# Attention and mixture of experts: whole-token scratch with one gather a tile, and single indirect transfers in the attention

## The chip, the cores and the metric

The kernel runs on one core of a Trainium2 chip. The metric is device time in microseconds (us): the median of several executions. The kernel before takes 1117.5 us (median of 3, 1113.73 to 1119.49).

The core's engines are TensorE (PE, with its weight loads as PEld), VectorE (DVE), ScalarE (ACT), GpSimd (POOL) and SyncE (SP), which issues most of the DMAs. Each engine takes its instructions in the order of the program; between engines they wait for one another by semaphores.

## The reference

```python
# q, k, v: 8 batches x 8 heads x 576 x 64
mask_plain = (rel >= 0) & (rel < 32)                      # heads 0..3
mask_dil = (rel >= 0) & (rel < 128) & (rel % 4 == 0)      # heads 4..7
attn = softmax(where(mask, q @ k.T / 8, -1e9))
x = (attn @ v).transpose(0, 2, 1, 3).reshape(4608, 512)   # one row a token

logits = x @ w_gate                                       # 8 experts
noisy = logits + log1p(exp(x @ w_noise)) * noise
top2 = argpartition(-noisy, 2, axis=1)[:, :2]
w = softmax(noisy[top2])
out = 0
for e in range(8):
    for k in range(2):
        m = top2[:, k] == e
        out[m] += w[m, k] * (relu(x[m] @ w1[e]) @ w2[e])  # 512 -> 1024 -> 512
```

## The kernel before, in words

**Attention.** The 8 batches make four units of two, and each unit has a dilated group (heads 4 to 7) and a plain one (heads 0 to 3). Each group is worked in three steps, 24 in all. A loop of 26 rounds, each with two half steps, works several steps at once in a pipeline. For a step, `qk` (L345) computes the scores on PE (L362); VectorE takes the maximum (L367) and subtracts it (L368) into a tile `a`, of which there is one; `expo` is ScalarE's exponential (L373); `ptr` transposes on PE (L387) and copies on ScalarE (L388); `pv` multiplies by v on PE (L405) and divides on VectorE (L412 to L417) into a tile `x`; `store_x` sends `x` from SP to a scratch in device memory, `xs` (L430, L432). `x_transpose` (L440) and `gate_mm` (L462) give the gate's logits, which ScalarE copies to their tokens' columns (L467 for plain heads, L488 for dilated ones).

The scratch of before has 9216 rows of 256 numbers: half a token each (the plain half or the dilated one), in the order in which the steps make them. `setup_b` (L220 to L252) computes on VectorE, from a token's number, the rows of its two halves, and `tokc` holds both.

**The table.** Generators run beside the attention, some instructions at a time. They pick each token's two experts, count their places, and write an entry (the two rows, the weight, the token) into a table `tab` in device memory, sorted by expert. `fill_slots` (L619) does that on GpSimd, with one indirect DMA of 128 rows for each of 36 token tiles and each of the two choices: 72 scatters. Those of the second choice go through a list, `backlog`, and are popped from it when there is room.

**The pace of the indirect transfers.** `new_slot` gives a number of turns at every half step: 4, 0, 4, 0 and so on. Each scatter of the table and each tile's gather in the attention takes one turn, in `pool_turn`. Ahead of the transfer, `pace` puts a tiny instruction on GpSimd: for the first turn of a slot a copy of one element of the latest `x` into `spacer` (L297), so that GpSimd waits there until that `x` exists, and for the other turns a memset (L299), which waits for nothing of PE or VectorE.

**Experts.** For each of the 8 experts, up to 1216 token rows are worked in three blocks of 3, 4 and 2 or 3 tiles of 128. `up` (L802) multiplies by w1 on PE (L814), with the relu on ScalarE (L818) into `hh` and the rest of a split into two parts on VectorE (L820); `down` (L841) multiplies by w2 (L856, and L850 and L852 for a last short tile), scales on VectorE (L865), and GpSimd adds the rows to the output with an indirect DMA (L833). Weights are loaded by SP into staging tiles `ws`, two of each kind (L686 for w1, L700 for w2), then split by ScalarE and VectorE.

Rows for expert 0 are gathered in the attention's last part, two indirect DMAs a tile (L758, one for each half token), and transposed on PE. Those of a later expert are gathered with four indirect DMAs a tile (L766), each of 32 tokens by four quarters of 128 numbers, so that the tile lies ready for VectorE's transposes in squares of 32 (L783), ScalarE's copy (L785) and VectorE's subtraction (L786). Their indices are loaded by SP (L735, L738, L740) and worked out on GpSimd (`idx_copy`, L742).

**A planner** sets the order in the experts: `plan` (L884) puts a function at a time in us of PE work, and `tick` (L892) advances that clock after each group of matmuls and emits what is due. `plan_x` (L794) plans, for a block's tile, its gather at a time t and its split at t + `LAG` (15). During expert 0 a function `some` gives one turn in each of the first 36 us to the rest of the table's scatters, and the backlog follows behind.

Of the kernel before, what the change touches and what calls it, by code (L numbers as in the profile page):

```python
# [41 lines left out]
LAG = 15  # L42
US_X = (17, 52)
# [3 lines left out]
def attention_moe_kernel(ctx, tc, qt, kp, kd, vpl, vdl, w_gate, w_noise, noise, w1, w2, out, CAPS=(1216, 1216, 1216, 1184, 1184, 1152, 1152, 1152), SPLITS=(0, 384, 896)):  # L47
# [49 lines left out]
    VD = dp.tile([128, 2, 9, 4, 2, 65], F32, name="vd")  # L97
# [15 lines left out]
    def v_loads(g):  # L113
        u, ty = g // 2, 1 - g % 2
        if ty:
            d = VD.rearrange("p w j h y c -> p w (j h y c)")
# [61 lines left out]
    for ty in range(2):  # L178
        eng = vector if ty == 1 else gpsimd
        m = acon.tile([128, 18, 64], BF, name=f"mask{ty}")  # L180
        eng.tensor_copy(m, m0[:, 0:1].to_broadcast([128, 18, 64]))
        if ty == 1:
            for blk, kd_ in {0: 1, 9: 1, 4: 2, 13: 2, 5: 3, 14: 3}.items():
                eng.tensor_copy(m[:, blk], m0[:, kd_])
        else:
            for x in range(2):
                for h in range(2):
                    p0 = 64 * x + 32 * h
                    eng.tensor_copy(m[p0:p0 + 32, 6 * h], m0[p0:p0 + 32, 1])
        masks.append(m)  # L190
# [29 lines left out]
    def setup_b():  # L220
# [3 lines left out]
        gpsimd.iota(tokc[:, :, 3:4], pattern=[[128, NT], [0, 1]], base=0, channel_multiplier=1)  # L224
        t = tokc[:, :, 3]
        v, s, i0, z, a = (acon.tile([128, 2, NT], I32, name=f"tc{i}") for i in range(5))
        gpsimd.iota(v[:, 0].rearrange("p (s j) -> p s j", j=3), pattern=[[0, 12], [128, 3]], base=0, channel_multiplier=1)
        vector.tensor_scalar(a[:, 0], t, 2, None, op0=OP.bitwise_and)
        vector.tensor_scalar(v[:, 1], t, 2, None, op0=OP.logical_shift_right)
        vector.scalar_tensor_tensor(v[:, 1], a[:, 0], 72.0, v[:, 1], op0=OP.mult, op1=OP.add)  # L230
        for u in range(U):
            c = slice(NG * u, NG * u + NG)
            gpsimd.iota(s[:, 0, c].rearrange("p (s j) -> p s j", j=3), pattern=[[384, 3], [0, 3]],
                        base=384 * (6 * u + 3), channel_multiplier=0)
            vector.tensor_scalar(a[:, 0, c], t[:, c], float(TU * u + S), 144.0, op0=OP.is_ge, op1=OP.mult)
            vector.scalar_tensor_tensor(v[:, 1, c], v[:, 1, c], -288.0 * u, a[:, 0, c], op0=OP.add, op1=OP.add)
            vector.memset(s[:, 1, c], 2304 * u)
        for lim in (192.0, 384.0):
            vector.tensor_scalar(z[:, int(lim) // 384], v[:, 1], lim, None, op0=OP.is_ge)
        vector.tensor_tensor(z[:, 0], z[:, 0], z[:, 1], op=OP.add)  # L240
        vector.scalar_tensor_tensor(s[:, 1], z[:, 0], 384.0, s[:, 1], op0=OP.mult, op1=OP.add)
        vector.tensor_scalar(a[:, 0], t, 1, None, op0=OP.bitwise_and)
        vector.tensor_tensor(z[:, 0], a[:, 0], z[:, 0], op=OP.subtract)
        vector.scalar_tensor_tensor(v[:, 1], z[:, 0], 192.0, v[:, 1], op0=OP.mult, op1=OP.add)

        vector.tensor_tensor(i0, v, s, op=OP.add)
        vector.tensor_scalar(a, v, 31, None, op0=OP.bitwise_and)
        vector.tensor_tensor(i0, i0, a, op=OP.add)
        vector.tensor_scalar(a, v, 32, None, op0=OP.bitwise_and)
        vector.scalar_tensor_tensor(i0, a, -31.0 / 32, i0, op0=OP.mult, op1=OP.add)  # L250
        for c in range(2):
            vector.tensor_copy(tokc[:, :, c], i0[:, c])  # L252
# [26 lines left out]

    gens, early = [], [True]  # L280
    room, held, rate = [0], set(), [1]
# [12 lines left out]
    def pace(yes=True):  # L294

        if yes and late["x"] is not None:
            gpsimd.tensor_copy(spacer, late["x"])  # L297
# [3 lines left out]
    def pool_turn():  # L301


        pace(fresh[0] and not experts[0])
# [31 lines left out]
    def blocks(st, ty):  # L336

        for r in range(6):
            a, jp = divmod(r, 3)
            b, ub = divmod(12 * st + 2 * r, 18) if ty == 0 else divmod(6 * st + 2 * jp, 9)  # L340
            yield r, a, jp, b, ub

    SB, PE_, PT, XG, XT, GS = {}, {}, {}, {}, {}, {}

    def qk(k):  # L345
# [8 lines left out]
        for e in range(6):  # L354
            for qd in range(4):
                if ty == 0:
                    x = qd // 2
                    b, ub = divmod(12 * st + 6 * (qd % 2) + e, 18)
# [10 lines left out]
        SB[k] = a  # L369

    def expo(k):
        p = sm.tile([128, 6, 64, 2], F32, name="pe")
        scalar.activation(p.rearrange("p j c w -> p j w c"), SB.pop(k).rearrange("p y (j w) c -> p (y j) w c", w=2),  # L373
                          AF.Exp, scale=0.125)
# [16 lines left out]
    def pv(k):  # L391
        g, st = divmod(k, 3)
        ty = 1 - g % 2
        pt = PT.pop(k)
        o = aps.tile([128, 2, 512], F32, name="o", tag="o")
        for hh in range(4):
            for r, a, jp, b, ub in blocks(st, ty):
                qd, c0 = (r, hh) if r < 4 else (2 * (r - 4) + hh // 2, 4 + hh % 2)
                if ty == 0:
                    y, src = hh // 2, 2 * (hh % 2) + a  # L400
                    rhs = VP[b][:, :, ub // 2, hh]
                else:
                    y, src = a, hh
                    rhs = VD[:, :, 3 * st + jp, hh, y]
                tensor.matmul(o[32 * qd:32 * qd + 32, c0 // 3, 130 * (c0 % 3):130 * (c0 % 3) + 130],  # L405
                              lhsT=pt[:, y, 128 * jp + 32 * src:128 * jp + 32 * src + 32],
# [14 lines left out]
        late["x"] = x[0:1, 0, 0, 0:1]  # L421
# [4 lines left out]

# [795 lines left out]
```

## Time and profile before

| | |
|---|---|
| device time, median of 3 (range) | 1117.5 us (1113.73 to 1119.49) |
| span of the profiled execution | 1109.4 us |
| PE busy | 1015.0 us, 91% |
| POOL busy | 527.7 us, 48% |
| DVE busy | 463.9 us, 42% |
| ACT busy | 319.8 us, 29% |
| moved by DMA | 132.91 MB, mean 120 GB/s |

The span reaches from the first instruction to the last in one profiled execution, and it is the time that the views divide. A row of the table of stretches gives, for a window of the span, each engine's busy time with its count of instructions in brackets, then the clock that the throttle granted to PE (1.00 is full speed), the mean busy share of the 16 DMA engines, and GB/s. A row of the timeline gives the start, the duration, the engine, the line, the operation, the tiles and their shapes, and in square brackets how long the engine was idle ahead of it and what released it. A row of the groups by line gives the count, then busy time and mean duration in ns, then the idle time ahead of the group's instructions and its main releaser.

### The profile page before, as it was taken

What the parts mean: (1) busy time and instruction counts of PE and PEld (TensorE: products, weight loads), DVE (VectorE), ACT (ScalarE), POOL (GpSimd) and SP (SyncE); (2) the same over time, 40 slices, a digit from 0 to 9 for tenths busy, and PEclk for the clock granted to TensorE, in tenths of its full rate; (3) what the DMA queues carried; (4) which work ended last, traced back from release to release, by engine and by line L of the source; (5) the groups of instructions that cost most, each with busy time, mean ns of one, the idle gap of its engine ahead of it and who ended that gap; (6) DMA issues with size and microseconds to landing.
All of it is one profiled execution on the core that took longest, in us unless ns stands there. A gap on an engine that the chain in (4) does not pass through costs nothing. (4 is left out here: it accounts for less than half of the span.)

```text
span 1109.4 us, 18401 instructions
## 1 busy us (share of the span) xinstructions
PE 1015.0 (91%) x7278; PEld 853.6 (77%) x7279; DVE 463.9 (42%) x1060; ACT 319.8 (29%) x612; POOL 527.7 (48%) x723
## 2 busy tenths in 40 slices
PE   5896776686999899999999999999999999999996
PEld 3774655465779789878988898788978898888885
DVE  6773535644224444334433433434343344333221
ACT  6673433531113232222222222212231213222110
POOL 6004243356866545664635564455456455553112
PEclk9998887887999999999999999999999999999999
DMA  7798687465243432633353334333433443353123
GB/s 275 254 345 292 193 270 251 122 205 161 44 90 76 102 101 48 139 60 103 65 117 68 97 72 101 82 79 85 97 83 81 104 68 102 62 129 58 32 30 46
DMA packets 77530, 132.91 MB, mean 120 GB/s; under 512 B 29968, under 2 KB 39616, under 8 KB 76160
## 3 DMA queue, kind: packets, MB, share of 16 engines
q1 hardware_dynamic: 55088, 92.55, 26.3%
q0 software_dynamic: 22352, 39.15, 19.6%
q8 instruction: 58, 0.95, 0.4%
q14 instruction: 32, 0.26, 0.1%
HBM read 92.11 MB, written 39.54 MB: 119 GB/s over the span
## 5 line engine op out<-in xcount | busy, mean ns | idle before, releaser
L814 PE MATMUL up<-x,w1h 128*128 128x512 f32 (+4 forms) x1536 | 397.5, 345 | 8.8 <-DVE hl L820 5.8
L766 POOL DMA_INDIRECT g<-xs,ixi x258 | 264.5, 1025 | 84.5 <-issue 79.1
L814 PEld LDWEIGHTS up<-x,w1h 128*128 128x128 f32 x1536 | 272.7, 189 | 36.4 <-DVE hl L820 7.6
L814 PE MATMUL up<-x,w1l 128*128 128x384 f32 (+4 forms) x768 | 264.1, 344 | 1.8 <-DVE w1l L696 1.1
L856 PE MATMUL dn<-w2h,hh 128*128 128x512 f32 x576 | 226.7, 394 | 2.0 <-DVE y L865 1.3
L856 PE MATMUL dn<-w2h,hl 128*128 128x512 f32 x576 | 225.3, 391 | 1.1 <-issue 1.1
L856 PE MATMUL dn<-w2l,hh 128*128 128x512 f32 x576 | 225.5, 391 | 0.6 <-issue 0.6
L820 DVE SCALAR_TENSOR_TENSOR hl<-up,hh 128x384 fp32r<-128x384 f32 (+2 forms) x192 | 106.1, 556 | 228.0 <-ACT hh L818 177.1
L833 POOL DMA_INDIRECT out_rows<-y,ixs x67 | 107.8, 1609 | 189.3 <-DVE y L865 158.3
L818 ACT ACTIVATE hh<-up 128x384 fp32r<-128x384 f32 (+4 forms) x192 | 94.2, 498 | 274.7 <-PE up L814 193.9
L814 PEld LDWEIGHTS up<-x,w1l 128*128 128x128 f32 x768 | 145.7, 190 | 14.7 <-DVE w1l L696 1.8
L856 PEld LDWEIGHTS dn<-w2h,hh 128*128 128x128 f32 x576 | 109.0, 189 | 25.6 <-DVE y L865 2.4
L856 PEld LDWEIGHTS dn<-w2h,hl 128*128 128x128 f32 x576 | 108.8, 189 | 24.0 <-issue 1.1
L856 PEld LDWEIGHTS dn<-w2l,hh 128*128 128x128 f32 x576 | 109.0, 189 | 22.6 <-issue 0.8
L865 DVE TENSOR_SCALAR y<-dn,ixs 128x512 f32<-128x512 f32 x63 | 46.9, 748 | 143.4 <-PE dn L856 114.9
L785 ACT CAST x<-xr 128x512 fp32r<-128x512 f32 x67 | 40.5, 605 | 189.9 <-DVE xr L783 158.5
L619 POOL DMA_INDIRECT tab<-en,si x72 | 72.2, 1002 | 30.7 <-issue 16.4
L696 DVE TENSOR_TENSOR w1l<-ws,w1h 128x1024 fp32r<-128x1024 f32 x32 | 38.8, 1217 | 94.8 <-ACT w1h L694 61.6
L297 POOL COPY spacer<-hh 1x1 f32<-1x1 f32 x72 | 24.2, 336 | 102.0 <-ACT hh L818 101.7
L694 ACT CAST w1h<-ws 128x1024 fp32r<-128x1024 f32 x32 | 33.0, 1048 | 115.9 <-DMA ws<-in_moe_w 115.8
L786 DVE TENSOR_TENSOR x<-xr,x 128x512 fp32r<-128x512 f32 x67 | 44.7, 666 | 18.0 <-ACT x L785 15.9
L783 DVE STREAM_TRANSPOSE xr<-g 128x512 f32<-128x512 f32 x67 | 45.7, 682 | 0.0
(184 smaller groups left out, 856.0 us busy)
## 6 DMA issues: line engine op xcount, KB each, us to landing
ws<-in_moe_w SPq DMA_DIRECT2D x64, 512.0 KB
out_rows<-zero SPq DMA_DIRECT2D x38, 256.0 KB
vd<-in_vdl SPq DMA_DIRECT2D x24, 390.0 KB
vp<-in_vpl SPq DMA_DIRECT2D x16, 585.0 KB
qt<-in_qt SPq DMA_DIRECT2D x14, 576.0 KB
xs<-x SPq DMA_DIRECT2D x24, 256.0 KB
kt<-in_kd SPq DMA_DIRECT2D x16, 320.0 KB
g<-xs,ixi POOLq DMA_INDIRECT x258
```

What stands on the lines that cost most here:

```text
L619: ins = gpsimd.indirect_dma_start(out=tab, out_offset=bass.IndirectOffsetOnAxis(ap=si[:, kq, t:t + 1], axis=0), in_=en[:, kq, t], in_offse ...
L696: return lambda: vector.tensor_tensor(b, s, a.bitcast(F32), op=OP.subtract)
L766: gpsimd.indirect_dma_start(out=g[:, j], out_offset=None, in_=xq, in_offset=bass.IndirectOffsetOnAxis(ap=IX[e][1][:, r0 // 32 + j:r0 // 32 ...
L783: vector.transpose(xr[:, :, 0:rn].rearrange("p c (g t) -> p g c t", t=32), g[:, 0:n].rearrange("p g (c d) -> p g c d", d=32))
L785: scalar.copy(xh[:, :, o:o + rn], xr[:, :, 0:rn])
L786: return lambda: vector.tensor_tensor(xl[:, :, o:o + rn], xr[:, :, 0:rn], xh[:, :, o:o + rn].bitcast(F32), op=OP.subtract)
L814: tensor.matmul(p[:, 0:n], lhsT=a[:, 128 * f:128 * f + 128], rhs=b[:, kc, 0:n], start=(i == 0), stop=(i == 11))
L818: scalar.activation(hh[:, f, 0:n], p[:, 0:n], AF.Relu)
L820: vector.scalar_tensor_tensor(hl[:, f, 0:m], p[:, 0:m], 0.0, hh[:, f, 0:m].bitcast(F32), op0=OP.max, op1=OP.subtract)
L833: ins = gpsimd.indirect_dma_start(out=out, out_offset=bass.IndirectOffsetOnAxis(ap=sc[0:rn, t, 1:2], axis=0), in_=y[0:rn], in_offset=None, ...
L856: tensor.matmul(p[0:rn], lhsT=a[:, f, o:o + rn], rhs=b[:, f % 2], start=(i == 0), stop=(i == 23))
L865: vector.tensor_scalar(y[0:rn], p[0:rn], wsc, None, op0=OP.mult)
```

## The change

**Scratch.** `xs` has 4608 rows of 512 numbers: whole tokens, in their own order. An entry of the table holds the token's number, so that `setup_b` loses its chain on VectorE. The host lays out q, k and v so that a step's output falls on such rows: the plain stores stay 3 DMAs a step, and the dilated ones are 3 or 4. The copies of the gate's logits become contiguous for plain heads, and those of dilated heads go from 56 to 32.

**Gather, hop.** A tile is gathered with one indirect DMA of whole tokens into `gr` (3 buffers). For expert 0 this tile is transposed on PE as before. For the later experts, SP stores it into a piece of device memory, `hop` (3 buffers; `send`, L715), and loads it back with four DMAs as squares of 32 tokens into `g` (2 buffers; `fetch`, L724). `plan_x` plans the send 4.0 us after the gather and the fetch 7.5 us after it; the split stays at `LAG`, 15, and is 11 and 13 for expert 1's first two blocks. Each split counts its rows in `full`, and before a block's `up` the planner's clock is advanced until its rows are all split. Index loads take a whole tile `ix` of table entries, and `idx_copy` goes.

**Pace.** In the attention each half step has one turn (`new_slot(1)`), and the transfer stands behind a copy of one element of `late["e"]`: the latest of `a` (set in `qk`), `x` (in `pv`) and, in the experts, `hh` (in `up`). In the experts every third turn has that copy, and the others a memset. `some` gives a turn for each 1.4 us of the planner's clock, over 78 us. The backlog is also popped in the experts, and expert 1's index load is planned 78.2 us after expert 0's start, where it stood at 42.

**First weights.** w1 of the experts is laid out by the host in the order in which the kernel loads it, so that `stage_w1` reads contiguous blocks.

The core of the diff:

```diff
-    xs = dram.tile([6 * U * 384, 256], F32, name="xs")
-    xq = xs.rearrange("r (q d) -> (r q) d", d=128)
+    xs = dram.tile([T, DM], F32, name="xs")
+    hop = ctx.enter_context(tc.tile_pool(name="hop", bufs=3, space=DRAM))
...
-            while room[0] > 0 and backlog and not experts[0]:
+            while room[0] > 0 and backlog:
...
-        pace(fresh[0] and not experts[0])
+        pace(fresh[0] if not experts[0] else turns[0] % 3 == 0)
+        turns[0] += experts[0]
...
+        late["e"] = a[0:1, 0, 0, 0:1]
...
-        late["x"] = x[0:1, 0, 0, 0:1]
+        late["e"] = x[0:1, 0, 0, 0:1]
...
+        gpsimd.indirect_dma_start(out=g[0:rn], out_offset=None, in_=xs[0:rows],
+                                  in_offset=bass.IndirectOffsetOnAxis(ap=IX[e][0:rn, t, 0:1], axis=0))
...
+    def send(e, t):
+        m = hop.tile([128, DM], F32, name="hop")
+        sync.dma_start(m[0:rn], GT[e, t][0:rn])
+    def fetch(e, t):
+        g = gp_.tile([128, 4, 128], F32, name="g", bufs=GBUFS[1])
+        for c in range(4):
+            sync.dma_start(g[32 * c:32 * c + 32, 0:rn // 32],
+                           m[0:rn, 128 * c:128 * c + 128].rearrange("(j t) d -> t j d", t=32))
...
+            plan(t + step * i + US_HOP[0], lambda ti=ti: send(e, ti))
+            plan(t + step * i + US_HOP[1], lambda ti=ti: fetch(e, ti))
...
-        new_slot((4, 0)[kb % 2], 1 if kb < 28 else 2)
+        new_slot(1, 1 if kb < 28 else 2)
...
+    def some(us=1.0):
+        credit[0] += us / US_POOL
+        if credit[0] >= 1:
+            credit[0] -= 1
+            new_slot(1)
...
+                while full.get((e, bi), 0) < BLS[e][bi][3]:
+                    tick(240)
```

On GpSimd in the attention, the first scatters of the table stand before like this (COPY is the spacer that waits for `x`, MEMSET the spacer that waits for nothing of PE or VectorE):

```order
L297 COPY spacer<-x 1x1
L619 DMA tab<-en_1453,si_1521 37376x4
L299 MEMSET spacer 1x1
L619 DMA tab<-en_1453,si_1521 37376x4
L299 MEMSET spacer 1x1
L619 DMA tab<-en_1453,si_1521 37376x4
L299 MEMSET spacer 1x1
L619 DMA tab<-en_1453,si_1521 37376x4
L297 COPY spacer<-x 1x1
```

The same place in the changed kernel:

```order
L273 COPY spacer<-x 1x1
L592 DMA tab<-en_1407,si_1475 37376x4
L273 COPY spacer<-x 1x1
L592 DMA tab<-en_1407,si_1475 37376x4
L273 COPY spacer<-a 1x1
L592 DMA tab<-en_1407,si_1475 37376x4
L273 COPY spacer<-x 1x1
L592 DMA tab<-en_1407,si_1475 37376x4
L273 COPY spacer<-a 1x1
```

Four scatters behind one wait have become one scatter behind each wait, by turns for `x` and for `a`.

On SP, between the loads of one expert's weights and the next index load, stands before (`ws` are staging tiles of weights, `ixt` and `ixs` the pieces of the index tile):

```order
L686 ISA
L686 DMA ws<-in_moe_w 128x1x1024
L735 ISA
L735 DMA ixt<-tab 32x37x2
L738 ISA
L738 DMA ixs<-tab 128x9x2
L740 ISA
L740 DMA ixs<-tab 32x2
L700 ISA
L700 DMA ws_6223<-in_moe_w 128x2x512
```

And in the changed kernel:

```order
L659 ISA
L659 DMA ws<-in_moe_w 128x1024
L715 DMA hop<-gr 128x512
L724 DMA g<-hop 32x4x128 x4
L659 ISA
L659 DMA ws<-in_moe_w 128x1024
L659 ISA
L659 DMA ws<-in_moe_w 128x1024
L715 DMA hop<-gr 128x512
L724 DMA g<-hop 32x4x128 x4
L715 DMA hop<-gr 128x512
L724 DMA g<-hop 32x4x128 x4
```

The sends and fetches of the hop now stand between the weight loads in SP's one order.

More of the change, by code (lines that the diff above doesn't have):

```diff
@@ L186, in attention_moe_kernel @@
             for x in range(2):
[L187 to L189 removed]
+                for b in range(2):
+                    eng.tensor_copy(m[64 * x:64 * x + 32, 7 * b], m0[64 * x:64 * x + 32, 1])
         masks.append(m)
@@ L223, in setup_b @@
         gpsimd.memset(tokc, 0)
[L224 to L252, printed above, removed]
+        for c in (0, 3):
+            gpsimd.iota(tokc[:, :, c:c + 1], pattern=[[128, NT], [0, 1]], base=0, channel_multiplier=1)
     def setup_c():
@@ L278, in setup_c @@
             at(6 + 6 * i, lambda i=i: pads(NR * i // 3, NR * (i + 1) // 3))
+    late["e"] = None
     gens, early = [], [True]
-    room, held, rate = [0], set(), [1]
+    room, held, rate, turns = [0], set(), [1], [0]
     fresh, backlog = [True], []
@@ L294, in pace @@
     def pace(yes=True):
-        if yes and late["x"] is not None:
-            gpsimd.tensor_copy(spacer, late["x"])
+        if yes and late["e"] is not None:
+            gpsimd.tensor_copy(spacer, late["e"])
         else:
@@ new lines, in new_idx, with idx_dma, gather @@
+        IX[e] = ixp.tile([128, nt, TC], I32, name="ix")
+    def idx_dma(e, a, b, base=None):
+        ti, n = IX[e], b - a
+        src = tab[a:b] if e == 0 else tab[bass.ds(EID[e] * ET if base is None else base, n)]
+        t, k = a // 128, n // 128
+        if k:
+            sync.dma_start(ti[:, t:t + k], src[0:128 * k].rearrange("(g t) c -> t g c", t=128))
+        if 128 * k < n:
+            sync.dma_start(ti[0:n - 128 * k, t + k], src[128 * k:n])
+    X, GT, full = {}, {}, {}
+    def gather(e, t):
+        rn = TLS[e][t][1] if e != "o" else 128
+        g = gp_.tile([128, DM], F32, name="gr", bufs=GBUFS[0])
+        rows = T
+        if e == 0:
+            rows = TU * (next((i for i in range(U - 1) if sum(TLS[0][t]) <= SPLITS[i]), U - 1) + 1)
+        elif e != "o":
+            pace()
+        gpsimd.indirect_dma_start(out=g[0:rn], out_offset=None, in_=xs[0:rows],
+                                  in_offset=bass.IndirectOffsetOnAxis(ap=IX[e][0:rn, t, 0:1], axis=0))
+        GT[e, t] = g
@@ L806, in up @@
         xh, xl = X_
+        assert full.pop(key if type(key) is tuple else (key, 0)) == n
         m = n - stacked
@@ L940, in split_first @@
     def split_first(bi, t):
+        if (0, t) not in GT:
+            later(1, lambda: split_first(bi, t))
+            return
         xsplit(0, bi, t)()
@@ L1032, in attention_moe_kernel, with drain @@
     gens.append(gate(33, 3))
-    def some():
-        new_slot(1)
+    credit = [0.0]
+    def some(us=1.0):
[3 more added lines that the diff above has]
+            new_slot(1)
+        else:
+            held.clear()
         micro(6)
-    def drain():
-        while gens:
-            some()
+    def drain(all):
+        while gens or (all and backlog):
+            some(US_POOL)
     actx.close()
-    late["x"] = None
+    late["e"] = None
     late["wp2"] = ctx.enter_context(tc.tile_pool(name="wp2", bufs=1, reuse_waits="tile"))
@@ L1158, in attention_moe_kernel @@
                 idx_dma("o", 0, 128, r0 + s0)
-                idx_copy("o", 0, 128)
                 gather("o", 0)
+                send("o", 0)
+                fetch("o", 0)
                 new_x("o", 0)
@@ L1211 @@
     given = _layouts(inputs["q"], inputs["k"], inputs["v"])
-    given.update((name, inputs[name]) for name in _NAMES)
+    given.update((name, _first_weights(inputs[name]) if name == "moe_w1" else inputs[name]) for name in _NAMES)
     for name, a in given.items():
```

212 lines of the change are left out of this document (79 added, 133 removed).

## The prediction, before the run

> **What bounds the kernel now.** First the page's head and a table of stretches: when is TensorE (PE) full, and at what clock?
>
> ```profile
> span 1109.4 us, 18401 instructions
> ```
>
> ```profile
> core 0: us, PE busy (x) PEld busy (x) DVE busy (x) ACT busy (x) POOL busy (x), PEclk, DMA share, GB/s
> 16.00:89.00 73.00, 65.87 (x1483) 53.36 (x1482) 51.78 (x177) 45.91 (x114) 5.99 (x23) 1.00 0.89 305
> 89.00:236.00 147.00, 100.55 (x1632) 74.62 (x1624) 66.58 (x245) 62.72 (x155) 55.34 (x97) 0.83 0.67 212
> 236.00:365.00 129.00, 117.14 (x558) 99.09 (x557) 49.38 (x161) 25.25 (x47) 86.32 (x129) 0.93 0.45 117
> 461.00:570.00 109.00, 106.73 (x522) 91.64 (x521) 45.87 (x75) 27.53 (x46) 61.74 (x77) 1.00 0.41 89
> ```
>
> From 461 on PE is busy 98% of the time at clock 1.00: the later experts are PE work, and nothing but a new wait changes them. The loose time lies earlier. The attention's second part, 89 to 236, has PE busy 68% of the time, at clock 0.83. Expert 0 (236 to 365) takes 129 us where a later expert with about as many matmuls takes 109. So I look at the attention's beat: each of its 24 steps has one L367, read from VectorE's timeline.
>
> ```profile
> 59.10 0.96 DVE L367 TENSOR_REDUCE mx<-s 128x12 f32<-128x768 f32 x1 [1.03 <-PE s L362]
> 65.11 0.96 DVE L367 TENSOR_REDUCE mx<-s 128x12 f32<-128x768 f32 x1 [1.04 <-PE s L362]
> ...
> 89.32 0.96 DVE L367 TENSOR_REDUCE mx<-s 128x12 f32<-128x768 f32 x1 [0.37 <-PE s L362]
> 109.35 0.96 DVE L367 TENSOR_REDUCE mx<-s 128x12 f32<-128x768 f32 x1 [6.30 <-PE xtp L440]
> 114.84 0.96 DVE L367 TENSOR_REDUCE mx<-s 128x12 f32<-128x768 f32 x1 [1.04 <-PE s L362]
> 125.76 0.96 DVE L367 TENSOR_REDUCE mx<-s 128x12 f32<-128x768 f32 x1 [5.90 <-remote]
> 135.68 0.96 DVE L367 TENSOR_REDUCE mx<-s 128x12 f32<-128x768 f32 x1 [1.56 <-PE xtp L440]
> ...
> 146.21 0.96 DVE L367 TENSOR_REDUCE mx<-s 128x12 f32<-128x768 f32 x1 [0.18 <-PE s L362]
> 166.13 0.96 DVE L367 TENSOR_REDUCE mx<-s 128x12 f32<-128x768 f32 x1 [6.07 <-remote]
> 172.90 0.96 DVE L367 TENSOR_REDUCE mx<-s 128x12 f32<-128x768 f32 x1 [1.03 <-PE s L362]
> 189.46 0.96 DVE L367 TENSOR_REDUCE mx<-s 128x12 f32<-128x768 f32 x1 [8.89 <-remote]
> 196.94 0.95 DVE L367 TENSOR_REDUCE mx<-s 128x12 f32<-128x768 f32 x1
> 212.76 0.96 DVE L367 TENSOR_REDUCE mx<-s 128x12 f32<-128x768 f32 x1 [7.11 <-PE xtp L440]
> ```
>
> An undisturbed step takes 6.01 us (59.10 to 65.11). Six steps take 20.03, 10.92, 9.92, 19.92, 16.56 and 15.82 us. In each of them VectorE waits for a PE result that, by its own row, was ready long before. What runs meanwhile? The timeline of one of them, and the counts of the two kinds of indirect transfer on GpSimd (POOL), scatters of L619 first, gathers of L758 second, in 89 to 213 and in expert 0:
>
> ```profile
> 119.26 1.52 PE L362 MATMUL s<-kt,qt 128*32 128x128 f32 x48
> 119.95 0.97 POOL L619 DMA_INDIRECT tab<-en,si  x1 [0.51 <-issue]
> ...
> 121.23 0.96 POOL L619 DMA_INDIRECT tab<-en,si  x1 [0.22 <-issue]
> ...
> 123.77 0.97 POOL L619 DMA_INDIRECT tab<-en,si  x1 [0.23 <-issue]
> ...
> 125.87 0.86 ACT L388 COPY pt<-pp 128x512 f32<-128x512 f32 x2 [3.89 <-remote]
> ```
>
> ```profile
> 89.00:213.00 124.00, 37.75 (x38) 0.84 0.74 236
> 236.00:365.00 129.00, 27.83 (x28) 0.93 0.45 117
> ```
>
> ```profile
> 89.00:213.00 124.00, 5.83 (x6) 0.84 0.74 236
> 236.00:365.00 129.00, 14.39 (x14) 0.93 0.45 117
> ```
>
> L362 is done at 120.78, yet L367 starts at 125.76 and L388 at 125.87, about 1 us after the burst's last transfer (123.77 + 0.97). All 44 transfers (38 + 6) lie in those six steps and none in the others. The six steps sum to 93.17 us, 57.1 above 6 x 6.01: **1.30 us a transfer**, as long as the transfer and the gap behind it. What the engines share there the trace doesn't say.
>
> **The change part by part.** *Pacing in the attention.* Turns go from four every second half step to one in each, and each transfer stands behind a copy that waits for the step's `a` or `x`. By the order of the change, 29 transfers (26 scatters, 3 gathers) are paced so, where 44 + 6 ran before the first matmul of expert 0. What one transfer alone costs no row shows. Upper end: 1.30. Lower end: nothing, by the first transfer of the first burst, beside which PE's results came on time:
>
> ```profile
> 89.24 1.11 POOL L619 DMA_INDIRECT tab<-en,si  x1 [0.89 <-DVE si L616]
> ...
> 89.95 0.86 ACT L388 COPY pt<-pp 128x512 f32<-128x512 f32 x2 [0.30 <-PE pp L387]
> ```
>
> A gain is excluded, since the transfers help no other engine. In the burst at 119.95 the wait began beside the first transfer. Two transfers a step stand about 3 us apart instead of 1.28, and what waits has some slack (L367 waits 1.04 us for PE even when undisturbed), so I take 0.5, nearer to the early row. From 89.32 eleven undisturbed steps lead to 155.4. From the last L367 (212.76) to the first matmul of expert 0 it takes 22.9 us now, in which the last 6 of the 50 transfers lie (6 x 1.30 = 7.8), so 15.1 without them: 170.5. With 29 x 0.5 = 14.5: 185.0.
>
> ```profile
> 235.70 0.60 PE L814 MATMUL up<-x,w1h 128*128 128x384 f32 x2
> ...
> 365.25 0.51 PE L814 MATMUL up<-x,w1h 128*128 128x384 f32 x2
> ```
>
> *Index arithmetic and logit copies.* `setup_b` loses its VectorE chain, and the logit copies of the dilated heads go from 56 to 32 (4 units x 4 runs x 2).
>
> ```profile
> 28.89 0.18 DVE L228 TENSOR_SCALAR tc<-tokc 128x36 int32<-128x36 int32 x1
> ...
> 33.31 0.29 DVE L252 COPY tokc<-tc 128x36 int32<-128x36 int32 x2
> ```
>
> ```profile
> L488 ACT COPY gs<-pp 64x128 f32<-64x128 f32 (+2 forms) x56 | 12.5, 323 | 15.7 <-PE pp L462 15.6
> ```
>
> The chain stands for 4.7 us ahead of that step's own L412 and delays one step; I take 2 us of it, as setup_c stays. 24 copies x 0.323 = 7.8 us come off ScalarE, which has slack in a step that PE fills; I take 1 us. Expert 0's first matmul then stands at 185.0 - 3 = 182. The stores change their rows, and the dilated ones go from 36 to 40; 4 issues are nothing on this queue.
>
> *What is late next:* the DMA engines. Between 89 and 236 they move 212 GB/s x 147 us = 31.2 MB, and this all stays. At the first part's rate, 305 GB/s at share 0.89 (343 at share 1), it takes 91 us: not before 180. With two limits so close I put the first matmul at 186: **49.7 us gained**.
>
> *Expert 0.* It takes 129.55 us (235.70 to 365.25) against 109 in 461 to 570, where PE ran 522 matmuls: 20.5 lost beside 28 + 14 = 42 transfers, 0.49 each. In the change 46 scatters and 7 gathers come here: 26 us at that price (upper end), nothing if the copies that wait for `hh` at every third turn break the bursts. I take 15: 124 us, **5.5 gained**. POOL must end them before expert 1's index load, planned 78.2 us of PE work in: 53 x 1.28 = 68 us and five output scatters. It just does.
>
> *Gather and hop.* A later tile costs POOL one gather instead of four:
>
> ```profile
> L766 POOL DMA_INDIRECT g<-xs,ixi x258 | 264.5, 1025 | 84.5 <-issue 79.1
> ```
>
> That frees some 190 us of POOL, which gives nothing, as PE doesn't wait for it. The hop puts a store and four loads a tile on SP's queue, behind one another, among the weight loads. A small load that waits for nothing else took this long to be usable:
>
> ```profile
> 174.79 0.54 SPq L731 DMA_DIRECT2D ixf<-tab  x1
> ```
>
> ```profile
> 177.76 1.00 POOL L758 DMA_INDIRECT g<-xs,ixf  x1 [6.30 <-DMA ixf<-tab]
> ```
>
> 3.0 us. Gather, send and fetch at 3 each are usable 10.5 us after the gather (sends are planned at 4.0, fetches at 7.5). The split is planned at 15, for expert 1 at 11 to 13. Later experts have their tiles tens of us ahead; expert 1 has 0.5 us to spare. I put **3 us lost** there, between 0 and 10. A send that waits on SP holds the weight loads behind it, and ScalarE's casts wait for those; POOL's copy of `a` makes the next step's L368 wait for POOL, once for some us where POOL waits for the index load (6.30). Both are in that range.
>
> The hop moves 67 x 0.5 MB = 34 MB more over 735 us, 46 GB/s beside 89 at share 0.41: about 0.62, so the cover holds. The Trainium skill ("DMA: Bandwidth & Descriptors", Issuing engines are not separate DMA queues) speaks against the change here: DMAs of SP and POOL run on the same 16 engines. By that rule the hop slows the weight loads, and if PE felt it the gain would shrink by the fourth rival's price.
>
> *Sum:* -49.7 - 5.5 + 3 = -52.2. Span 1109.4 becomes 1057.2. The median of the runs shown, 1117.5, lies 8.1 above the span: **1065**. With one transfer at 0.1 to 1.0 us, expert 0 losing 5 to 26 and the hop 0 to 10, this case spans 1045 to 1090.
>
> **The rivals.** *A transfer costs the same wherever it stands.* Then 29 x 1.30 = 37.7: first matmul at 170.5 + 37.7 - 3 = 205.2, 30.5 gained. Expert 0 with 53 transfers loses 26 (135 us, 5.5 lost), the hop 3: 22 gained, **1095**. For it: the price equals the transfer's own time in bursts of 4 and of 12. Against: 89.95.
>
> *Single transfers are free.* The DMA bound of 180 holds the attention, 55.7 gained; expert 0 loses 3 (17.5 gained), the hop nothing: **1044**. For it: 89.95; against: the burst at 119.95.
>
> *The bursts aren't the cause*, only fall together with some other wait of those steps. Then transfers are moved and nothing else: 3 us gained, 3 lost, **1117**. The Trainium skill ("SBUF — State Buffer", SBUF: two separate sides) says that DMA and compute ports are disjoint and neither slows the other. By that rule this case is the likely one; the rows speak against it, as six of six steps with transfers are long and no other one by more than 3.5 us.
>
> *The hop on SP delays the weights* (the other side). SP is in order: a send waits for its gather and a fetch for its send, with the next weight block's load behind them. If that makes each of the 7 later experts start 10 us late, 52.2 gained less 70: **1135**; it decides from 52.2 / 7 = 7.5 us each. For it: expert 1's spare 0.5 us. Against: tiles and weights of later experts are planned ahead by more than the 3 us steps, and DMA share stays near 0.62.
>
> **How the numbers follow.** Forecast 0.55, same price 0.17, free 0.08, bursts not the cause 0.07, weights late 0.13. A difference of 0.5% (5.6 us) is about what a measurement of this kernel can tell from no change. Faster: 0.55 + 0.17 + 0.08 = 0.80; the same 0.07; slower 0.13. The range 1042 to 1108 holds the first three cases with their costs' bounds and leaves 0.20 out.
>
> **What would show it.** L367 about 6 to 7 us apart to the end of the attention, with no wait of 5 us in brackets; the first matmul of expert 0 near 186; PE's clock in that stretch back near 1.00 and DMA share above 0.8; expert 0 near 124 us; expert 1's first matmul without a wait for a tile; later experts at 105 to 109. It is wrong if steps with single transfers last 7.5 us or more (same price), if they stay at 10 to 20 (not the cause), or if PE is idle for several us ahead of each expert's first matmul (weights late).

## The result, and the profile after

The changed kernel takes 1065.5 us (median of 4, 1060.95 to 1069.18) where the kernel before takes 1117.5 (median of 3; a fourth run, of 2525 us, is not counted): ratio 0.9536, 95% interval 0.9481 to 0.9591. The profiled execution has a span of 1062.3 us. Forecast were 1065 and a span of 1057.2, so the span is 5 us longer than forecast and the time beside it 5 us shorter; that the median agrees to half a microsecond is luck.

One thing must be known to read the later numbers: the kernel before took 1113 to 1121 us in some sessions and 1049 to 1050 us in others, the same through each session, and one chip showed both; I call these sessions *with the hold* (the two first profiles belong there) and *without* it, for a reason that the first experiments show, and compare within one kind unless I say otherwise.

The stretches of the changed kernel from 89 us on, cut at the first matmuls of expert 0 and expert 1, with one later expert behind (columns as in the prediction's first table):

```profile
span 1062.3 us, 18626 instructions
89.00:194.00 105.00, 85.55 (x1621) 66.37 (x1620) 66.31 (x245) 62.85 (x142) 39.32 (x63) 0.94 0.90 297
194.00:327.00 133.00, 116.12 (x559) 98.81 (x557) 49.35 (x160) 25.77 (x47) 78.20 (x132) 0.94 0.47 126
425.00:531.00 106.00, 106.00 (x522) 92.09 (x522) 46.06 (x75) 27.21 (x45) 30.54 (x40) 1.00 0.55 140
```

The attention's second part took 147 us at clock 0.83 before and takes 105 at 0.94 now, with the DMA engines at share 0.90. Expert 0 is no shorter. VectorE's timeline of the changed kernel (the maxima, L337 now), and PE's of the first matmuls of experts 0 and 1:

```profile
97.08 0.96 DVE L337 TENSOR_REDUCE mx<-s 128x12 f32<-128x768 f32 x1 [1.55 <-PE pp L359]
103.52 0.96 DVE L337 TENSOR_REDUCE mx<-s 128x12 f32<-128x768 f32 x1 [1.99 <-PE s L332]
...
154.16 0.95 DVE L337 TENSOR_REDUCE mx<-s 128x12 f32<-128x768 f32 x1
162.95 0.92 DVE L337 TENSOR_REDUCE mx<-s 128x12 f32<-128x768 f32 x1
170.48 0.94 DVE L337 TENSOR_REDUCE mx<-s 128x12 f32<-128x768 f32 x1
193.45 0.99 PE L777 MATMUL up<-x,w1h 128*128 128x384 f32 x2
327.23 0.69 PE L777 MATMUL up<-x,w1h 128*128 128x384 f32 x1 [4.91 <-ACT x L742]
```

The steps are 6 to 9 us long and none waits 5 us in brackets: the six long ones are gone. Their sum, from 97.08 to 170.48, is 73.4 us for ten steps, 7.3 each, not 6.0. Five of these ten last 7.5 us or more, which the prediction named as the sign of its first rival (the same price everywhere); experiment 4 has steps of 7.2 to 8.2 us without any scatter, so that they don't show it. Of the other signs, the DMA share (0.90) and the later experts (106 us) came true; the first matmul near 186, the clock near 1.00, expert 0 near 124 us and expert 1 without a wait did not.

Against the profile of before the span splits so: expert 0's first matmul 42.3 us earlier (235.70 to 193.45), expert 0 up to expert 1's first matmul 4.2 longer (133.8 for 129.6), everything behind it 9.1 shorter (1062.3 - 327.2 = 735.1 for 1109.4 - 365.2 = 744.2). Forecast were 49.7 earlier, 5.5 shorter and 3 longer: two of the three signs are wrong.

The new row [4.91 <-ACT x L742] is expert 1 waiting for its first tile. PE's waits of the changed kernel between 194 and 330 (in total, times, longest):

```profile
PE xrp L737 <- DMA gr<-xs,ix: 5.8, 1, 5.8
PE up L777 <- ACT x L742: 4.9, 1, 4.9
PE up L777 <- DVE hh L786: 4.9, 3, 4.2
PE up L777 <- DVE x L744: 1.8, 1, 1.8
```

5.8 us for a gathered tile of expert 0, 4.2 for a part of `hh` that ScalarE and VectorE made late, in a run of transfers, 4.9 and 1.8 for expert 1's tiles: 16.7 us in which PE stands still, where the copies and the hop were forecast to cost 3.

### The profile page after: what moved, and what is told of

Its sections match the earlier page's. It is cut to its first block, busy times and chain, and to the rows that moved or that the text cites. A ratio compares the mean times of both kernels' runs of the same rounds, so it can differ in the third digit from the quotient of the medians.

```text
span 1062.3 us, 18626 instructions
## 1 busy us (share of the span) xinstructions
PE 1000.6 (94%) x7278; PEld 850.4 (80%) x7279; DVE 463.0 (44%) x1031; ACT 321.6 (30%) x588; POOL 330.3 (31%) x490
## 5 line engine op out<-in xcount | busy, mean ns | idle before, releaser
L777 PEld LDWEIGHTS up<-x,w1h 128*128 128x128 f32 x1536 | 276.1, 191 | 39.2 <-ACT x L742 5.4
L796 POOL DMA_INDIRECT out_rows<-y,ix x77 | 127.1, 1650 | 230.7 <-DVE y L828 212.4
L828 DVE TENSOR_SCALAR y<-dn,ix 128x512 f32<-128x512 f32 x72 | 54.0, 749 | 196.2 <-PE dn L819 190.3
L742 ACT CAST x<-xr 128x512 fp32r<-128x512 f32 x67 | 40.6, 605 | 218.1 <-DVE xr L740 208.4
L707 POOL DMA_INDIRECT gr<-xs,ix x77 | 86.8, 1127 | 48.2 <-issue 28.8
L679 ACT CAST w2h<-ws 128x1024 fp32r<-128x1024 f32 x32 | 33.5, 1046 | 39.3 <-DMA ws<-in_moe_w 39.3
```

The costliest lines, as they stand in the source:

```text
L707: gpsimd.indirect_dma_start(out=g[0:rn], out_offset=None, in_=xs[0:rows], in_offset=bass.IndirectOffsetOnAxis(ap=IX[e][0:rn, t, 0:1], axis=0))
L742: scalar.copy(xh[:, :, o:o + rn], xr[:, :, 0:rn])
L777: tensor.matmul(p[:, 0:n], lhsT=a[:, 128 * f:128 * f + 128], rhs=b[:, kc, 0:n], start=(i == 0), stop=(i == 11))
L796: ins = gpsimd.indirect_dma_start(out=out, out_offset=bass.IndirectOffsetOnAxis(ap=sc[0:rn, t, 1:2], axis=0), in_=y[0:rn], in_offset=None, ...
L828: vector.tensor_scalar(y[0:rn], p[0:rn], wsc, None, op0=OP.mult)
```

## The experiments

**1. Bursts back in the attention.** The changed kernel with the old rhythm alone:

```diff
-        late["e"] = a[0:1, 0, 0, 0:1]
...
-        new_slot(1, 1 if kb < 28 else 2)
+        new_slot((4, 0)[kb % 2], 1 if kb < 28 else 2)
```

> The changed kernel with the old rhythm in the attention: four turns in every second half step, one copy of x ahead of the first of them, and none of a. Theory (bursts of indirect transfers on GpSimd hold up PE's results): the six long steps of 10 to 20 us come back, expert 0's first matmul goes from 193.5 to 230 to 236, expert 0 itself gets a little shorter since fewer transfers are left for it, and the time is 1095 to 1110 us. Rival (the new order of scratch, stores and copies brought the gain, the bursts only fell together with another wait): first matmul stays within 5 us of 193.5, time 1060 to 1072.

It took 1044.5 us, 0.9947 (0.9921 to 0.9974) of the kernel before, which took 1049.9 on that chip. The steps that the bursts made long are gone, though the bursts are back. By its letter neither side has won: the first matmul at 186.66 is 6.8 us away from 193.5, where the rival allowed 5, and the time is below both ranges. One step is still long, the last (17.33 us), and in it PE waits for gathered tiles of expert 0 (5.1 and 1.2 us); the kernel before has the same step in a session without the hold (15.43 us, experiment 6). But the kernel before had lost its long time there too, so the run says something else. The timeline of this kernel (L332, L358, L337, L359 as before; L591 are the scatters):

```profile
98.15 0.97 POOL L591 DMA_INDIRECT tab<-en,si  x1 [0.22 <-issue]
98.24 0.87 PE L358 MATMUL pp<-ident,pe 128*128 128x128 f32 x6
98.36 0.96 DVE L337 TENSOR_REDUCE mx<-s 128x12 f32<-128x768 f32 x1 [1.04 <-PE s L332]
98.98 0.86 ACT L359 COPY pt<-pp 128x512 f32<-128x512 f32 x2
99.43 0.97 POOL L591 DMA_INDIRECT tab<-en,si  x1 [0.21 <-issue]
186.66 0.60 PE L776 MATMUL up<-x,w1h 128*128 128x384 f32 x2
```

Within a run of twelve scatters ScalarE takes PE's result as soon as it begins to appear. Nothing is held here.

**2. The same kernel in a session with the hold.**

> The kernel of the first experiment again (the changed kernel with four turns in every second half step), since that one ran on a chip where the kernel before takes 1050 us, and a third chip has now shown 1121 for it. If this run meets a chip of the 1120 kind, the theory (bursts of indirect transfers hold PE's results there) expects the long steps of 10 to 20 us, a first matmul at 225 to 240 and 1090 to 1115 us, 0.97 to 0.99 of the kernel before; the rival (the other parts brought the gain) expects a first matmul under 200 and 0.95. If it meets a chip of the 1050 kind, both expect 1044 us again, 0.995.

Here the kernel before took 1113.1 us and this one 1087.2: 0.9765 (0.9725 to 0.9805). The same kernel at nearly the same place:

```profile
98.14 2.79 PE L332 MATMUL s<-kt,qt 128*32 128x128 f32 x48
99.42 0.98 POOL L591 DMA_INDIRECT tab<-en,si  x1 [0.51 <-issue]
...
100.86 0.96 PE L358 MATMUL pp<-ident,pe 128*128 128x128 f32 x6
...
103.26 0.97 POOL L591 DMA_INDIRECT tab<-en,si  x1 [0.22 <-issue]
105.12 0.96 DVE L337 TENSOR_REDUCE mx<-s 128x12 f32<-128x768 f32 x1 [5.79 <-remote]
105.23 0.86 ACT L359 COPY pt<-pp 128x512 f32<-128x512 f32 x2 [5.08 <-remote]
224.97 0.60 PE L776 MATMUL up<-x,w1h 128*128 128x384 f32 x2
```

PE's scores are done at 100.93 and its transposes at 101.8, by the ends that the profile models; VectorE and ScalarE go on at 105.1 and 105.2, 0.9 us after the end of the burst's last transfer (104.23). The long steps of 10 to 19 us are back, as the theory had it; first matmul (224.97) and time lie just under its ranges. So pacing is worth 224.97 - 193.45 = 31.5 us of the 42.3 in a session with the hold; 6.3 of them go again in expert 0 (133.8 us against 127.5). The other 10.7 (235.70 to 224.97) come from the other parts.

"PE's results are held" is too narrow, though. In the burst just before, eight transfers from 85.98 to 96.06, PE itself stands still between groups of a few matmuls, and the profile shows nothing that it waits for ("issue"). The first burst in the profile of before has the same:

```profile
93.11 0.38 PE L451 MATMUL pp<-xt,wg 128*32 128x128 f32 x3 [1.00 <-issue]
94.55 0.44 PE L451 MATMUL pp<-xt,wg 128*32 128x64 f32 x3 [1.06 <-issue]
```

```profile
95.06 0.38 PE L405 MATMUL o<-vp,pt 128*32 128x130 f32 x3 [1.10 <-issue]
```

Between 85 and 236, such waits of PE come to 18.0 us in 32 pieces here and to 2.6 in 3 in experiment 1; in the kernel before they are 17.0 in 26 with the hold and 6.4 in 5 without (experiment 6). Whether PE's results become visible late, or whether these engines get their own next instructions late, no run separates.

**3. Pacing alone in the kernel before.**

```diff
         SB[k] = a
+        late["x"] = a[0:1, 0, 0, 0:1]
...
-        new_slot((4, 0)[kb % 2], 1 if kb < 28 else 2)
+        new_slot(1, 1 if kb < 28 else 2)
```

> The kernel before with the pacing alone: one turn in each half step, behind a copy of the latest a or x; half-token scratch, two gathers a tile and four for later experts stay. Theory: expert 0's first matmul moves from 235.7 to 192 to 202, expert 0 takes 130 to 140 us since more transfers are left for it in bursts, time 1080 to 1095 us. Rival (the other parts brought the gain): first matmul stays above 225, time above 1105.

It ran without the hold: 1071.9 us, 1.0229 (1.0177 to 1.0282). The first matmul comes at 190.39 and expert 1's at 328.90:

```profile
190.39 0.60 PE L815 MATMUL up<-x,w1h 128*128 128x384 f32 x2
...
328.90 0.51 PE L815 MATMUL up<-x,w1h 128*128 128x384 f32 x2
```

Expert 0 lasts 138.5 us, 23 more than in the kernel before of experiment 6 (115.8): 34 transfers lie ahead of the first matmul where it was 50, so that many more run in expert 0, and ScalarE waits 20 us there for a tile of expert 1 that is gathered behind them. Without the hold pacing only moves transfers to a place where they are in the way. With the hold this kernel was not run, so that neither the theory nor the rival was put to its test.

**4. No scatters at all.** `fill_slots` returns without its indirect DMA (the table stays padding, so the gathers fetch the first 128 tokens).

> The changed kernel without any of the 72 scatters of table entries (left out: the table keeps its padding rows, so all gathers fetch the first 128 tokens over and over; everything else runs as before). Gives what the scatters still cost. If single transfers still cost 0.5 us each in the attention: first matmul from 193.5 to about 180 (13 to 15 us earlier), expert 0 from 133.7 to 112 to 118, time 1030 to 1040. If single transfers are free: first matmul stays at 190 to 194, and only expert 0 gets shorter, time 1045 to 1052. If the DMA engines bind the attention: first matmul not before 180.

1046.4 us, 0.9962 (0.9934 to 0.9991), without the hold. The first matmul is where "0.5 us each" had it, the time where "free" had it (1045 to 1052): expert 0 still takes 123.9 us, not 112 to 118. Its first matmul is the base on which the transfers' price stands, and its waits in expert 0, with the gather behind the first of them, show what the scatters are not to blame for:

```profile
181.87 0.59 PE L772 MATMUL up<-x,w1h 128*128 128x384 f32 x2
201.77 0.97 POOL L702 DMA_INDIRECT gr<-xs,ix  x1 [9.71 <-DMA out_rows<-zero]
PE xrp L732 <- DMA gr<-xs,ix: 5.8, 1, 5.8
PE up L772 <- ACT x L737: 4.6, 1, 4.6
```

Without any scatter PE waits 5.8 us for expert 0's gathered tile and 4.6 for expert 1's first, nearly as in the changed kernel (5.8 and 4.9). The late gather follows an index load that SP issues at 195.45 among stores of zeros to the output, where the DMA engines are full (share 1.00 from 195 to 209).

With the hold, 29 scatters ahead of the first matmul in the changed kernel cost (193.45 - 181.87) / 29 = 0.40 us each, 47 in bursts (224.97 - 181.87) / 47 = 0.92. Without the hold it is (189.30 - 181.87) / 28 = 0.27 and (186.66 - 181.87) / 47 = 0.10. The base is of a session without the hold; experiment 9 has 180.54 with it, which makes the first two prices 0.45 and 0.95.

**5. Four indirect gathers a tile again** in experts 1 to 7 (three extra ones of 128 rows by 32 numbers behind each tile's own, into a tile that nobody reads).

> The changed kernel with three more indirect gathers behind each tile's own in experts 1 to 7 (128 rows of 32 numbers each into a tile that nobody reads): four indirect gathers a tile as in the kernel before. The changed kernel's experts 1 to 7 take 726.4 us from their first matmul to the last one's end, 8.1 less than before. Theory (fewer indirect gathers gave these 8 us): 6 to 10 us come back, time 1071 to 1076. Rival (the 8 us have another source, the loads of w1 in one piece for example): time within 3 us of 1065.

1057.0 us, 1.0071 (1.0039 to 1.0102), without the hold, where the changed kernel has 1.0019 in another session. That is some 5.5 us, just under what the theory had, but the place is another:

```profile
318.96 0.69 PE L783 MATMUL up<-x,w1h 128*128 128x384 f32 x1 [13.45 <-ACT x L748]
```

Expert 1 waits 13.45 us for its first tile, and from there to the end it takes 1055.6 - 319.0 = 736.6 us, as in the changed kernel (735.1). In this run more gathers hurt where a tile is late already, and not behind; what shortened the later experts is not shown by it.

**6. Both kernels as they are,** on one chip.

> The kernel before itself, unchanged, with a profile beside those of the other runs. In the runs on another chip of the first four experiments the kernel before took about 1050 us where it had taken 1118, and a kernel with bursts of five scatters lost nothing by them. Theory (the hold-up of PE's results during GpSimd's transfers belongs to the chip or the session in which the first profiles were taken): here six of six steps with bursts are about 6 to 7 us long, expert 0's first matmul comes at 180 to 190 and the time is 1045 to 1055 us. Rival (the hold is always there in this kernel and the first four experiments were in some other state): first matmul at 235, time 1110 to 1120.

> The changed kernel itself, unchanged, on the same chip as the kernel before. If the hold is missing there, pacing gains nothing: first matmul at 187 to 193, and expert 0 with its late expert 1 (5 to 12 us) makes it the slower of the two or the same: ratio 1.00 to 1.01, 1050 to 1060 us. If the hold is there, ratio 0.95 as in the first measurement.

1049.0 us for the kernel before and 1051.6 for the changed one, ratio 1.0019 (0.9995 to 1.0044): without the hold the change is worth nothing. The times are those expected. The kernel before misses two of the theory's signs: its first matmul comes at 198.28, not at 180 to 190, and two steps last 9.91 and 15.43 us, the second of them the last one, in which PE waits for gathered tiles. Its stretches and first matmuls:

```profile
89.00:198.00 109.00, 88.13 (x1668) 69.25 (x1666) 68.35 (x251) 64.40 (x158) 57.10 (x98) 0.91 0.90 284
198.00:314.00 116.00, 112.28 (x562) 96.47 (x563) 49.62 (x161) 25.67 (x48) 85.39 (x128) 0.99 0.51 133
198.28 0.99 PE L814 MATMUL up<-x,w1h 128*128 128x384 f32 x2
314.12 0.51 PE L814 MATMUL up<-x,w1h 128*128 128x384 f32 x2
```

And the changed one, first matmuls and PE's waits from 190 to 330:

```profile
189.30 0.99 PE L777 MATMUL up<-x,w1h 128*128 128x384 f32 x2
318.06 0.69 PE L777 MATMUL up<-x,w1h 128*128 128x384 f32 x1 [6.84 <-ACT x L742]
PE xrp L737 <- DMA gr<-xs,ix: 6.4, 1, 6.4
PE up L777 <- DVE x L744: 1.8, 1, 1.8
```

The attention ends 9.0 us earlier, expert 0 lasts 128.8 us instead of 115.8, 13.0 longer, and the rest is 2.0 shorter (735.1 for 737.2, by the spans of 1053.2 and 1051.3). The waits of 6.8 and 6.4 lie in expert 0's stretch and make 13.2 us, the size of its loss; the 1.8 lies behind it. With the hold the same places have 4.9, 5.8 and 1.8.

**7. No hop.** The gathered tile goes straight to VectorE's transposes (its tokens then stand in a wrong order), with five gather buffers; sends and fetches are gone.

```diff
-            plan(t + step * i + US_HOP[0], lambda ti=ti: send(e, ti))
-            plan(t + step * i + US_HOP[1], lambda ti=ti: fetch(e, ti))
```

> The changed kernel without the hop: a gathered tile goes straight to VectorE's transposes (so the tokens stand in a wrong order, with the same work on every engine), 5 gather buffers. If the hop costs what was forecast, 3 us (0 to 10), all of it at expert 1's start, the time is 1 to 8 us below the changed kernel's on the same chip and later experts do not change. Rival (SP delays the weights): more than 10 us below, spread over the experts.

1041.6 us, 0.9919 (0.9894 to 0.9944) beside 1.0019 of the changed kernel in the same session, without the hold: 10.0 us. Its expert 1 and waits:

```profile
307.60 0.33 PE L778 MATMUL up<-x,w1h 128*128 128x384 f32 x1
PE xrp L740 <- DMA gr<-xs,ix: 5.9, 1, 5.9
PE up L778 <- DVE x L747: 2.3, 1, 2.3
```

The wait of 6.84 is gone and 2.3 is left. From expert 1's third block on (367.17 here, 380.07 with the hop) both kernels take 673.1 us: the hop costs at expert 1's start and in its first blocks, and the rival (SP delays the weights of every expert) is out. The 10.0 us are those of the hop with its three gather buffers against five without it; the two were not taken apart.

**8. No copies of `hh`** ahead of the transfers in expert 0: memsets only.

> The changed kernel with no copy of hh ahead of any of the table's scatters or expert 0's gathers in the experts (memsets alone, as before). Theory (GpSimd's wait for hh, 10.43 us in the profile of the changed kernel, makes expert 0's second block of gathers late, 5.8 us of idle PE at 220, and with it the index load of expert 1): 5 to 12 us faster than the changed kernel on the same chip, where bursts are harmless; where bursts are held, 0 to 10 us slower.

1051.5 us, 1.0012 (0.9987 to 1.0038), no different from the changed kernel's 1.0019. PE still waits 7.3 us for the gathered tile. GpSimd no longer waits for `hh`, but a scatter into the table waits 16.0 us ahead of that gather, by the profile for the stores of zeros. The theory falls.

**9. Neither scatters nor stores of zeros in the attention,** so that the DMA engines have 5 MB less there (`NZERO = 0` on top of experiment 4).

> The changed kernel without the 72 scatters (as in the third experiment: gathers fetch the first 128 tokens over and over) and with all 38 stores of zeros to the output planned in expert 0 (19 of them were in the attention). Without scatters alone, expert 0's first matmul came at 181.9. Theory (the DMA engines set the end of the attention, as the forecast's floor of 180 had it): 5 MB less at 343 GB/s bring it up to 14 us forward, to 168 to 177; expert 0 then loses some of it to late stores. Rival (PE's own chain sets it): it stays at 179 to 183.

In a session with the hold (before: 1120.7) it took 1043.7 us, 0.9321 (0.9257 to 0.9384). Its first and last step of eleven, its first matmul, and the stretches from 145 on:

```profile
88.27 0.96 DVE L337 TENSOR_REDUCE mx<-s 128x12 f32<-128x768 f32 x1
...
162.20 0.95 DVE L337 TENSOR_REDUCE mx<-s 128x12 f32<-128x768 f32 x1
180.54 0.60 PE L772 MATMUL up<-x,w1h 128*128 128x384 f32 x2
145.00:165.00 20.00, 16.86 (x386) 13.80 (x375) 18.04 (x85) 15.23 (x35) 3.90 (x8) 1.00 0.63 212
165.00:182.00 17.00, 10.26 (x127) 7.99 (x128) 9.68 (x30) 11.13 (x24) 1.97 (x8) 1.00 0.54 174
```

With DMA at share 0.63 and 0.54 from 145 on the first matmul is still at 180.5, as the rival had it. Up to 145 the engines are as full as ever (share 0.93 to 1.01), but none of the waits that the profile lists for PE from 85 to 182 is for a DMA: the chain of PE, VectorE and ScalarE sets it, not the DMA engines. And a session with the hold loses nothing where no scatter runs. With experiment 2, in which only the bursts are different, this puts the loss on GpSimd's transfers. Whether other work on GpSimd of that length would do the same wasn't tried.

**10. Expert 1's index earlier.**

```diff
-US_POOL = 1.4
-US_ALL = 78
+US_POOL = 1.0
+US_ALL = 56
```

> The changed kernel with a turn for each 1.0 us of the planner's clock instead of 1.4, all of them over 56 us instead of 78, so that expert 1's index load and its gathers come 22 us of PE work sooner. In the changed kernel on the chip of the last four runs PE waited 6.8 + 1.8 us for expert 1's first tiles, and without the hop 2.3. Theory (the longer way of a tile, through the hop, finds no cover at expert 1 because its index load waits for the last scatter): both waits go, 6 to 12 us faster than the changed kernel where bursts are harmless (1040 to 1046 us, 0.987 to 0.995 of the kernel before); where GpSimd's transfers hold PE's results, denser scatters cost 0 to 10 us in expert 0. Rival (the wait has another cause, SP's weight loads ahead of the sends): 0 to 2 us.

With the hold: 1071.8 us, 0.9560 (0.9515 to 0.9604), beside 0.9536 of the changed kernel in the first session. Expert 0 and expert 1 start at

```profile
191.64 0.60 PE L777 MATMUL up<-x,w1h 128*128 128x384 f32 x2
...
338.97 0.50 PE L777 MATMUL up<-x,w1h 128*128 128x384 f32 x2
```

and expert 1's waits are gone, as the theory had it. But expert 0 takes 147.3 us instead of 133.8, more than the 0 to 10 that were expected: its down block beside a run of 32 transfers lasts 39.9 us where it lasted 17.7. The one gain is paid with the other loss. There PE stands still ahead of one matmul after the other, waiting for nothing that the profile shows, while the DMA engines are almost idle (share 0.03 from 264 to 285):

```profile
280.56 0.58 PE L819 MATMUL dn<-w2l,hh 128*128 128x512 f32 x1 [2.21 <-issue]
PE dn L819 <- issue: 14.6, 11, 2.3
```

So the hold is not one of results alone, and it needs no full DMA engines. Without the hold this kernel was not run.

**11. Expert 0's index loads on GpSimd's queue** instead of SP's.

> The changed kernel with expert 0's two index loads issued from GpSimd's queue, behind the scatters they need, instead of SP's, where the second stands behind weight loads and stores of zeros. In the profiles of the changed kernel PE stands still for 5.8 to 6.4 us in expert 0's first down block for a gathered tile of the second block, whose scatter and gather follow that index load. Theory (SP's order makes the index load late, and PE pays): that wait goes and the kernel is 4 to 8 us faster than the changed kernel, 1044 to 1048 us on a chip where the kernel before takes 1050, 0.947 to 0.952 of it where that takes 1115 to 1120. Rival (the load is late because the copies of hh and the generators are, or the traffic of zeros delays it as well on any queue): within 2 us of the changed kernel, or slower since GpSimd now waits itself.

1048.9 us, 0.9989 (0.9964 to 1.0015), without the hold: against the changed kernel's 1.0019 (in another session) about 3 us, and the intervals overlap. PE's wait for the tile goes from 6.4 to 4.5, and the stretch around it reads:

```profile
203.00:216.00 13.00, 7.75 (x45) 6.82 (x43) 10.54 (x50) 3.46 (x6) 5.52 (x8) 0.97 1.02 360
PE xrp L738 <- DMA gr<-xs,ix: 4.5, 1, 4.5
```

The DMA engines are full (share 1.02) with the stores of zeros that SP issues from 204.9 on, and load and gather are slow in that traffic from whichever queue: mostly the rival. The Trainium skill ("DMA: Bandwidth & Descriptors", Issuing engines are not separate DMA queues) says that a DMA from another engine saves issue time only, and these rows agree. Experiment 9, which has all 38 stores of zeros in expert 0, waits 8.0 us for that tile, which fits too. That fewer zeros there would help wasn't tried: the output's first scatter-adds need them.

Of the complete kernels none is shown to beat both in both kinds of session. Without the hold the one with bursts does, by half a per cent (0.9947, experiment 1); with it none that was run is better than the changed kernel, and the intervals of experiment 10 and of the changed kernel overlap.

## Why the prediction was right, point by point

**Bursts hold PE's results: right about the bursts, where the profile of before was taken; too narrow about what is held.** Experiments 2 and 1 show the loss on one kernel with and without the hold, experiment 9 that it goes with the transfers. That VectorE waits in all six long steps for a PE result that was ready long before was read from one of them and does not hold for the first: there PE is late itself (95.06, after a standstill of 1.10 us), and experiment 10 has the same in expert 0. The third rival ("the bursts aren't the cause") is out in sessions with the hold; in the others it describes what happens, 1.0019. The Trainium skill ("SBUF — State Buffer", SBUF: two separate sides) has DMA and compute on disjoint ports; the sessions without the hold agree (bursts cost 0.10 us a scatter there). In those with it compute does stand still beside GpSimd's DMAs (0.92), and the measurement decides; that it is at these ports isn't shown. Nothing in the profile of before alone could tell that it showed one of two kinds of session.

**The price of a single transfer, 0.5: nearly right,** 0.40 to 0.45. The price in a burst, 1.30, was too high as a price of the transfer alone: 0.92 to 0.95 by experiment 2. It was taken above six steps of 6.01 us, too short a base.

**The undisturbed base, 170.5: wrong by 10 to 11 us.** I took eleven steps at 6.01 us and 15.1 us behind the last. Without any scatter eleven steps take 73.9 us (88.27 to 162.20, 6.7 each) and the way from the last L337 to expert 0 is 18.3: 180.5 (181.9 in experiment 4). A beat read at one early step was carried through steps that have more to do; the prediction's own list had one of 7.48 us without a transfer (189.46 to 196.94).

**The floor of 180 by the DMA engines: the number right, the reason wrong** (experiment 9). It lifted 182 to 186, nearer to the measured 193.45, for a cause that the runs don't show.

**Index arithmetic, copies, layout, 3 us: too small.** Without pacing the first matmul still comes 10.7 us earlier with the hold (235.70 to 224.97) and 11.6 without it (198.28 to 186.66). Which of the parts brings it was not taken apart.

**Expert 0, 5.5 us gained: wrong, 4.2 lost.** I counted transfers (53 for 42) and asked whether the copies break the bursts. They don't: 24 transfers stand in one run, and PE loses 4.2 us to a result held there. What I had not looked for is the way of a gathered tile of expert 0's second block, 5.8 us late. The scatters don't make it late: without any of them the wait is the same (experiment 4), and its index load stands among the stores of zeros. The 4.9 us ahead of expert 1 lie in this stretch too.

**The hop, 3 us in expert 1: place right, size wrong,** 10.0 by experiment 7, at the end of the range that I gave. "Expert 1 has 0.5 us to spare" left out how late the index load itself is planned, 78.2 us in, so that the whole chain comes late: with no scatter to wait for the tile is still 4.6 us late (experiment 4), and with the load planned 22 us sooner it is not (experiment 10). The rival of late weights had the right queue in mind and the wrong victim.

**Later experts, no gain from fewer gathers: wrong with the hold.** From expert 1's first matmul on the kernel before takes 744.2 us with the hold and 737.2 without, the changed kernel 735.1 in both. That 7 us of the 9.1 are bursts of four gathers held up fits this, but is argued: PE's waits behind that point are 10.4 us in the kernel before with the hold and 5.2 without, but experiment 5 met no session with the hold.

The errors of the span, +7.5 at the first matmul, +9.7 in expert 0 and -12.1 behind it, sum to +5.1; the 8.1 us beside the span were 3.2 in the runs after, which took these away. In the runs with both numbers on record a run's time is 1.6 to 2.4 us above its own span, so that the rest of the 8.1 was a quick execution in the profile of before, not a cost: here it happened to cancel a span forecast too short.

## What to carry to other kernels

Take the profile of before twice, in two sessions, before a change is built on one wait in it: here the same kernel has two times, 6% apart, and the change is worth 0.9536 in one and 1.0019 in the other. Where an engine is paced or its work moved, look for who is queued behind it at the new place: here expert 0's tile was late behind an index load among stores of zeros, and expert 1's behind an index load that the plan put too late. A run without the suspected work, like experiment 4, tells which waits it really makes. A stretch's undisturbed length is read from all its steps, or from a run with the disturbance taken out, not from one clean beat.

## What the runs showed of the hardware that was not expected

In sessions with the hold PE, VectorE and ScalarE fall behind beside GpSimd's runs of indirect transfers. VectorE and ScalarE take up PE's results only after a run ends, 0.9 us after the last of four (104.23 to 105.12), or PE itself stands for up to 2.3 us ahead of single matmuls, waiting for nothing that the profile shows (14.6 us in 11 pieces in experiment 10). In sessions without it the same program shows the result at once within a run of twelve. The mean granted clock of the kernel before is lower with the hold (0.955 to 0.970 against 0.979 to 0.993), but experiment 9, in such a session and without scatters, has 0.980 to 0.988: this speaks for a clock that follows the waits and doesn't make them. The hold is not a property of one chip by its number: one chip held in one session (1113.1 us for the kernel before) and did not in another (1048.9). What sets it stays open.
